# The small addition of 1e-9 to the softmax sums: on GpSimd instead of VectorE

## The chip, the core and the metric

The kernel runs on one core of a Trainium2 chip. The core has five engines with instruction queues of their own: TensorE (PE in the profile, its weight loads PEld), VectorE (DVE), ScalarE (ACT), GpSimd (POOL) and SyncE (SP, which here issues the DMAs). Each engine works through its queue in order, and engines wait for each other by semaphores. The metric is the device time of one execution in microseconds, lower is better.

## The reference

Sink attention with a sliding window feeds a layer of experts. The first part, with 4 batches, 8 heads, 768 positions and head size 64:

```python
scores = scale * np.matmul(q, k.transpose(0, 1, 3, 2))
keep = is_sink | in_window            # 4 sinks, window of 128
scores = np.where(keep, scores, -1e9)
scores = scores - np.max(scores, axis=-1, keepdims=True)
a = np.exp(scores)
a = a / (np.sum(a, axis=-1, keepdims=True) + 1e-09)
attn = np.matmul(a, v)
```

The second part takes the 3072 x 512 result `x`, forms gates `P` from `x @ w_gate` by eight rounds of row and column normalisation, and adds up eight experts: `out += P[:, e:e+1] * (relu(x @ w1[e]) @ w2[e])`.

## The kernel before

**Attention.** The work is cut into 48 units: 4 batches x 6 blocks of 128 positions x 2 halves of the heads, so a unit has 4 heads. A unit's scores are 128 queries by 260 columns a head: 4 sinks, the block before and the block itself. Values are split into a rounded part and a rest, so most products are three matmuls. The loop over `n` (lines 712 to 756) interleaves units: in round `n`, PE makes the scores of unit `n + 1`, transposes the queries and keys of unit `n + 2`, transposes the probabilities of unit `n`, and multiplies those of `n - 1` with the values. Between them it does pieces of the first expert (`run_fill`, `gate_step`).

**The work around the change** is in `scores(n, pr)`, called twice a unit, for heads 0 and 1 and for heads 2 and 3:

- L461, PE: six matmuls into two PSUM tiles of the pool `ps_st`, which has four;
- L464, DVE: scale, mask and row minimum of the negated scores, once a head;
- L467, ACT: the exponential, once a head; its row sums go to `sm`;
- L468: add 1e-9 to the two columns of sums, giving `rs` (128 partitions x 2);
- L469, DVE: the reciprocal of `rs`, in place;
- L471, GpSimd: multiply the 128x260 probabilities of each head by its column of `rs`.

Other lines that the prediction names: L430 and L431 split the transposed queries and keys (ACT rounds, DVE takes the rest); L350 is the same split for several things, among them the transposed probabilities `PT` and pieces of weights (`W`, `W2f`); L482 is PE's transpose of the probabilities; L604 and L605 are the activation of the first expert's hidden layer; L440 and L441 split `v` on GpSimd; L496 and L497 split the sinks' probabilities there; L403, L406 and L407 prepare the sinks' values once a batch; L532 copies the finished output, L540 and L541 split it.

The four tiles of `ps_st` are used eight times a round: four for scores, one for the transposed queries and keys, two for the transposed probabilities, one for the sinks. So a round's scores can be written only when L431, L350 and L501 of the round before have read their tiles.

**What sets the order.** In this stage only PE's order is the order of the code (`tc.manual_schedule(engines={PE})`, line 711). On DVE, ACT and GpSimd the framework's planner orders the instructions, by their place in the program and by its own estimate of when each can start. From line 1140 on all engines follow the code's order, and L468 does not occur any more.

**Afterwards** come the gates' normalisation, interleaved with the first expert, and then the experts' products for the rest of the span, in a form that needs seven block products where the plain one has eight.

Of the kernel before, what the change touches and what calls it, by code (L numbers as in the profile page):

```python
# [12 lines left out]
ALU = mybir.AluOpType  # L13
# [216 lines left out]
def tile_sink_attention_moe(ctx: ExitStack, tc: tile.TileContext, q, k, v, wg, w1, w2, out):  # L230

    nc = tc.nc
# [211 lines left out]
    def scores(n, pr):  # L444

        b, i, hh = units[n]
        u = us[n]
        K, Q = KQ[hh][:, :, :, 0:CW], KQ[hh][:, :, :, CW:][:, :, :, turn_of(b, i)]
        if pr == 0:
            u["sc"] = att.tile([P, HH, CW], F32, name="sc", bufs=3)  # L450
            u["st"] = att.tile([P, 3, HH], F32, name="st", bufs=3)
        sc = u["sc"]
        nmx, sm, rs = (u["st"][:, j, :] for j in range(3))
        hs = range(2 * pr, 2 * pr + 2)
        p2 = slice(2 * pr, 2 * pr + 2)
        ps = {h: ps_st.tile([P, CW], F32, name="st") for h in hs}

        for j, (a, c) in enumerate(((0, 0), (0, 1), (1, 0))):
            for h in hs:
                r0 = (h % 2) * D  # L460
                nc.tensor.matmul(ps[h], lhsT=Q[r0:r0 + D, a, pr, :], rhs=K[r0:r0 + D, c, pr, :],  # L461
                                 start=(j == 0), stop=(j == 2))
        for h in hs:
            nc.vector.tensor_tensor_reduce(out=sc[:, h, :], in0=ps[h], in1=masks[place(b, i).start, min(i, 2)], op0=ALU.add, op1=ALU.min,  # L464
                                           scale=-scale, scalar=3.0e38, accum_out=nmx[:, h:h + 1])
        for h in hs:
            nc.scalar.activation(sc[:, h, :], sc[:, h, :], AF.Exp, bias=nmx[:, h:h + 1], scale=-1.0, accum_out=sm[:, h:h + 1])  # L467
        nc.vector.tensor_scalar(rs[:, p2], sm[:, p2], 1e-9, None, op0=ALU.add)  # L468
        nc.vector.reciprocal(rs[:, p2], rs[:, p2])  # L469
        for h in hs:  # L470
            u["scaled"] = nc.gpsimd.tensor_scalar(sc[:, h, :], sc[:, h, :], rs[:, h:h + 1], 1.0, op0=ALU.mult, op1=ALU.mult).ins  # L471
# [239 lines left out]
    with tc.manual_schedule(engines={PE}):  # L711
        for n in range(-2, L + 3):
# [15 lines left out]
            if on(n + 1):  # L728
                scores(n + 1, 0)
                scores(n + 1, 1)  # L730
# [788 lines left out]
```

## Time and profile before

| | |
|---|---|
| time, median of 3 runs | 2141.11 us (2140.84 to 2141.45) |
| the profiled execution's own time | 2141.32 us |
| its span (first to last instruction) | 2139.5 us |
| busy in the span: PE, DVE, ACT, POOL | 2120.6, 1538.2, 883.0, 752.4 us |
| mean granted TensorE clock | 0.998 |

The times in the profile are those of one execution, in microseconds from the start of the span unless marked ns. A timeline row has the start, the duration, the engine, the line of the code, the operation, the tiles (written <- read) and a count; in brackets stands how long the engine was idle before it and who ended that. Consecutive instructions on one engine overlap a little, as the next starts before the one in front has written its last result. A row by line has a count and the smallest, median and largest duration in ns. A row of windows gives the stretch, its length, then busy time and count of PE, PEld, DVE, ACT and POOL, the granted clock, the share of DMA and GB/s. A row of the chain has the start, the time on the chain, the engine, tile and line.

### The profile page before, as it was taken

To read this page: it belongs to the slowest core of one execution; us is meant where nothing else is said; L and a number is where in the kernel's file an instruction comes from. 1 tells how busy PE (TensorE), PEld (TensorE's weight loads), DVE (VectorE), ACT (ScalarE), POOL (GpSimd) and SP (SyncE) were. 2 spreads that over 40 slices of the span, in tenths; PEclk is the share of its full clock that TensorE was granted. 3 is DMA by queue.
4 is the path that set the end of the run, shared out by engine and by line. 5 is a ranking of instruction groups with operands and counts; after the bars stand their busy time and mean duration, and the time that the engine had idled before them with its cause. 6 is when DMAs were issued, how large, how long until landed. Compare 5 with 4: busy or idle time off the path is not lost.

```text
span 2139.5 us, 31828 instructions
## 1 busy us (share of the span) xinstructions
PE 2120.6 (99%) x10501; PEld 1770.4 (83%) x10501; DVE 1538.2 (72%) x2821; ACT 883.0 (41%) x1867; POOL 752.4 (35%) x950
## 2 busy tenths in 40 slices
PE   8999999999999999999999999999999999999998
PEld 7898897888888888888888888888888888888887
DVE  9878878877777776766666666666656666676666
ACT  7777744444444444442333223332333223332222
POOL 7766643233232331232223222232423232233223
PEclk9999999999999999999999999999999999999999
DMA  7434326999998987686666666667866666666662
GB/s 184 96 81 103 85 80 223 320 300 315 295 315 286 313 287 251 219 278 209 201 191 204 206 193 205 202 200 260 300 205 194 200 206 193 201 207 189 205 197 85
DMA packets 397643, 453.83 MB, mean 212 GB/s; under 512 B 99680, under 2 KB 265760, under 8 KB 396576
## 3 DMA queue, kind: packets, MB, share of 16 engines
q1 hardware_dynamic: 397080, 451.57, 67.8%
q8 instruction: 86, 1.41, 0.3%
q14 instruction: 85, 0.70, 0.1%
q10 hardware_dynamic: 392, 0.16, 0.0%
HBM read 314.17 MB, written 137.46 MB: 211 GB/s over the span
## 4 chain that ended last, share of the span: by engine, by line
PE 93%; DVE 3%; ACT 2%; POOL 1%; issue 0%; DMA 0%; SPq 0%; DVEq 0%; ACTq 0%; POOLq 0%
PE c L784 41%; PE o L1343 20%; PE held L1343 8%; PE o L1028 7%; PE held L1028 7%; PE O L520 3%; PE st L461 2%; ACT sc L467 1%; PE o L615 1%; PE st L482 1%; PE g L599 1%; PE st L426 1%; DVE sc L464 0%; POOL sc L471 0%; DVE PT L350 0%
## 5 line engine op out<-in xcount | busy, mean ns | idle before, releaser
L810 ACT CAST hf<-w 128x512 fp32r<-128x512 f32 x448 | 265.5, 622 | 561.8 <-POOL w L1310 298.9
L1343 PE MATMUL o<-hf,W2q 128*128 128x512 f32 x1920 | 472.0, 389 | 0.0
L1343 PEld LDWEIGHTS o<-hf,W2q 128*128 128x128 f32 x1920 | 360.0, 188 | 75.5 <-DVE acc L1357 0.9
L784 PE MATMUL c<-T,W1q 128*128 128x512 f32 x1530 | 388.9, 389 | 0.2 <-DVE w L1291 0.2
L811 DVE TENSOR_TENSOR hf<-w,hf 128x512 fp32r<-128x512 f32 x448 | 329.3, 763 | 76.2 <-ACT hf L810 68.5
L784 PEld LDWEIGHTS c<-T,W1q 128*128 128x128 f32 x1530 | 286.8, 188 | 60.7 <-DVE w L1291 0.9
L1357 DVE TENSOR_TENSOR acc<-o,acc 128x512 f32<-128x512 f32 x298 | 204.7, 688 | 171.1 <-PE o L1343 171.1
L784 PE MATMUL c<-B,W1q 128*128 128x512 f32 x1134 | 278.3, 389 | 0.0
L1310 POOL TENSOR_TENSOR w<-w 128x512 f32<-128x512 f32 x64 | 82.7, 1293 | 491.6 <-DVE w L1292 491.6
L784 PEld LDWEIGHTS c<-B,W1q 128*128 128x128 f32 x1134 | 212.5, 188 | 44.0
L1291 DVE TENSOR_TENSOR w<-c,M 128x512 f32<-128x512 f32 x192 | 132.3, 689 | 138.0 <-PE c L784 132.6
L1287 ACT COPY M<-c 128x512 f32<-128x512 f32 x192 | 112.7, 587 | 249.4 <-PE c L784 249.3
L1343 PE MATMUL held<-hf,W2q 128*128 128x512 f32 x768 | 194.8, 389 | 0.0
L784 PE MATMUL c<-T,W1f 128*128 128x512 f32 x672 | 171.2, 390 | 0.1
L1028 PE MATMUL held<-W2f,h 128*128 128x512 f32 x672 | 171.1, 390 | 0.0
L1028 PE MATMUL o<-W2f,h 128*128 128x512 f32 x672 | 170.6, 389 | 0.1
L1343 PEld LDWEIGHTS held<-hf,W2q 128*128 128x128 f32 x768 | 144.0, 188 | 29.8
L1325 POOL TENSOR_TENSOR w<-w 128x512 f32<-128x512 f32 x64 | 106.3, 1661 | 176.0 <-DVE hf L811 176.0
L1028 PEld LDWEIGHTS o<-W2f,h 128*128 128x128 f32 x672 | 126.0, 188 | 27.0 <-DVE acc L1035 0.9
L784 PEld LDWEIGHTS c<-T,W1f 128*128 128x128 f32 x672 | 125.7, 188 | 27.0 <-issue 0.5
L1028 PEld LDWEIGHTS held<-W2f,h 128*128 128x128 f32 x672 | 125.8, 188 | 26.4 <-DVE W2f L811 0.5
L837 POOL TENSOR_TENSOR r<-r 128x256 f32<-128x256 f32 x27 | 20.1, 746 | 359.2 <-ACT M L991 223.1
(216 smaller groups left out, 3104.5 us busy)
## 6 DMA issues: line engine op xcount, KB each, us to landing
W2q<-w2s SPq DMA_DIRECT2D x448, 256.0 KB, 3.2
W1q<-w1s SPq DMA_DIRECT2D x444, 256.0 KB, 2.9
w1s<-W1f SPq DMA_DIRECT2D x56, 896.0 KB, 7.8
w2s<-WT SPq DMA_DIRECT2D x136, 256.0 KB, 3.5
r<-in_moe_w_dram SPq DMA_DIRECT2D x64, 512.0 KB, 3.9
w2s<-W2f SPq DMA_DIRECT2D x56, 256.0 KB, 4.8
PB<-psd SPq DMA_DIRECT2D x16, 512.0 KB, 4.1
w2s<-W2f SPq DMA_DIRECT2D x56, 128.0 KB, 6.5
```

The source lines that it names most:

```text
L461: nc.tensor.matmul(ps[h], lhsT=Q[r0:r0 + D, a, pr, :], rhs=K[r0:r0 + D, c, pr, :], start=(j == 0), stop=(j == 2))
L520: nc.tensor.matmul(u["O"][:, pr], lhsT=x_, rhs=y_, start=(j == 0), stop=(j == len(ops) - 1))
L784: nc.tensor.matmul(ps, lhsT=w1(a, k), rhs=x[:, b, k, :], start=(start and j == 0), stop=(stop and j == len(TERMS) - 1), skip_group_check=n ...
L810: nc.scalar.copy(dst[:, 0], src)
L811: at(1, lambda: nc.vector.tensor_sub(dst[:, 1], src, f32(dst[:, 0])))
L1028: nc.tensor.matmul(o, lhsT=h[c, th][:, a, off:off + P], rhs=W2F[n][:, w, c, :], start=(begin and c == 0 and j == 0), stop=(end and c == 1 ...
L1287: nc.scalar.copy(t, T["c2"])
L1291: nc.vector.tensor_add(w, T["c1"], T[m])
L1310: nc.gpsimd.tensor_sub(S3, T["A11"], T["A21"])
L1325: at(k, lambda: nc.gpsimd.tensor_sub(T["A11"], w, T["A11"]))
L1343: nc.tensor.matmul(o, lhsT=W2Q[part, n, m][:, a, k * P:(k + 1) * P], rhs=F[part, n, H_OF[m]][:, w, :], start=(j == 0 and (begin or not hol ...
L1357: nc.vector.tensor_add(sums[m, k], o, sums[m, k])
```

## The change

The addition at L468 goes from VectorE to GpSimd. There it is written with a second operation, a multiplication by 1.0, which leaves the value as it is. The reciprocal after it stays on VectorE and the scaling on GpSimd. Nothing else is edited.

```diff
         for h in hs:
             nc.scalar.activation(sc[:, h, :], sc[:, h, :], AF.Exp, bias=nmx[:, h:h + 1], scale=-1.0, accum_out=sm[:, h:h + 1])
-        nc.vector.tensor_scalar(rs[:, p2], sm[:, p2], 1e-9, None, op0=ALU.add)
+        nc.gpsimd.tensor_scalar(rs[:, p2], sm[:, p2], 1e-9, 1.0, op0=ALU.add, op1=ALU.mult)
         nc.vector.reciprocal(rs[:, p2], rs[:, p2])
         for h in hs:
             u["scaled"] = nc.gpsimd.tensor_scalar(sc[:, h, :], sc[:, h, :], rs[:, h:h + 1], 1.0, op0=ALU.mult, op1=ALU.mult).ins
```

## The prediction

> **What bounds the kernel now.** I read the page's chain of work that ended last first; then the windows that cut the span into stages; then inside the attention stage the views of single lines and the list of waits from 60 us on, the timeline of one steady round, and the chain of the first 44 us.
>
> ```profile
> PE 93%; DVE 3%; ACT 2%; POOL 1%; issue 0%; DMA 0%; SPq 0%; DVEq 0%; ACTq 0%; POOLq 0%
> ...
> 8.00:30.00 22.00, 19.39 (x107) 15.71 (x107) 20.85 (x80) 17.09 (x55) 18.48 (x40) 0.92 0.80 203
> 30.00:60.00 30.00, 28.70 (x247) 26.21 (x245) 27.83 (x100) 26.30 (x83) 21.85 (x53) 1.00 0.64 168
> ...
> 110.00:160.00 50.00, 50.00 (x431) 45.47 (x432) 38.51 (x142) 35.58 (x111) 29.01 (x69) 1.00 0.36 85
> ...
> L468 DVE TENSOR_SCALAR st<-st x96: 140/170/1282, 10.1 to 288.5; 128x2 f32<-128x2 f32 x96
> DVE KQ L431 <- ACT KQ L430: 3.8, 11, 1.0
> L431 DVE TENSOR_TENSOR KQ<-st,KQ x38: 670/692/694, 60.4 to 283.4; 128x512 fp32r<-128x512 f32 x38
> ```
>
> TensorE (PE) carries 93% of the chain, so time is lost or won only where PE waits. The window rows list busy time of PE, PEld, DVE, ACT and POOL. L468, the changed addition, runs 96 times, all before 289 us: the other 1850 us of the span have none of it and can only shift as a block. Within the first 289 us there are two stages. From 8 to 60 us VectorE (DVE) is busy 20.85 of 22 and 27.83 of 30 us: there it is as much the limit as PE. From 110 to 160 us PE is busy for all 50 us while DVE has 11 us free and GpSimd (POOL) 21 us: there PE is the limit. The last two rows, from 60 us on, are the waits of L431 and its count: 38 rounds, in 11 of which it waits for L430 on ScalarE (ACT); they come up below.
>
> One steady round, DVE first, then GpSimd, ACT and PE's weight loads:
>
> ```profile
> 120.03 0.17 DVE L468 TENSOR_SCALAR st<-st 128x2 f32<-128x2 f32 x1
> 120.24 0.17 DVE L469 RECIPROCAL st<-st 128x2 f32<-128x2 f32 x1
> 121.02 0.17 DVE L468 TENSOR_SCALAR st<-st 128x2 f32<-128x2 f32 x1 [0.62 <-ACT sc L467]
> 121.23 0.17 DVE L469 RECIPROCAL st<-st 128x2 f32<-128x2 f32 x1
> 121.31 0.41 DVE L605 SCALAR_TENSOR_TENSOR h<-g,h 128x256 fp32r<-128x256 f32 x1
> 121.76 0.69 DVE L431 TENSOR_TENSOR KQ<-st,KQ 128x512 fp32r<-128x512 f32 x1
> 122.37 1.28 DVE L350 TENSOR_TENSOR PT<-st,PT 128x512 fp32r<-128x512 f32 x2
> 120.58 1.93 POOL L471 TENSOR_SCALAR sc<-sc,st 128x260 f32<-128x260 f32 x4 [3.96 <-ACT sc L467]
> 119.81 0.19 ACT L467 ACTIVATION_READ_ACCUMULATOR sc<-sc,st 128x1 f32 x1
> 121.16 0.57 ACT L430 CAST KQ<-st 128x512 fp32r<-128x512 f32 x1
> 123.25 0.87 PEld L461 LDWEIGHTS st<-KQ 64*128 64x128 f32 x12 [0.37 <-DVE PT L350]
> 127.00 0.51 PEld L482 LDWEIGHTS st<-ident,sc 128*128 128x128 f32 x4
> ```
>
> A round does a pair of heads twice. The first pair's sums are ready at 119.81 + 0.19 = 120.00, which I call e. DVE adds, divides and ends at 120.41, and GpSimd scales from 120.58, e + 0.58. The second pair's sums come at e + 0.99; DVE had stood 0.62 us waiting for them. What follows on DVE is what PE needs: L431 and L350, whose results free the PSUM tiles that PE's next scores (L461) write. L431 starts at 121.76, e + 1.76, just after ACT's cast L430 ends at 121.16 + 0.57 = 121.73. In 11 rounds of 38 it even stands waiting for that cast. So in the steady stage the addition is not what L431 waits for.
>
> **The change, part by part.** Removed: 96 DVE instructions of 0.17 us median. Added: 96 GpSimd instructions of the same shape. Moved: the wait for ACT goes from DVE's queue to GpSimd's, and DVE's reciprocal L469 now waits for GpSimd, with L605, L431 and L350 queued behind it. On GpSimd the scalings L471 and then the splits of v (L440, L441) and of the sinks (L496, L497) are queued behind the addition; PE uses these a round or more later. No DMA is issued or moved.
>
> *The price of the addition on GpSimd.* The trace has no 128x2 addition there. The nearest rows are L496, 128x16, at 0.205 us, and on the far side a GpSimd fill of 128x4 at 0.10 us.
>
> ```profile
> L496 POOL TENSOR_SCALAR SS<-sc x80: 201/205/216, 21.6 to 290.3; 128x16 fp32r<-128x16 f32 x80
> L287 POOL MEMSET mask<- 128x4 f32 x1 | 0.1, 100 | 0.0
> 77.03 0.41 ACT L540 CAST B<-xr 128x256 fp32r<-128x256 f32 x1 [1.02 <-DVE xr L532]
> 77.52 0.74 POOL L541 TENSOR_TENSOR B<-xr,B 128x256 fp32r<-128x256 f32 x1 [0.28 <-ACT B L540]
> 81.81 0.74 POOL L441 TENSOR_TENSOR V<-vr,V 128x256 fp32r<-128x256 f32 x1
> 82.60 0.43 DVE L464 CUSTOM_DVE_ANT_0 sc<-st,mask 128x260 f32<-128x260 f32 x1 [0.16 <-POOL V L441]
> ```
>
> I take 0.20 us, the same kind of instruction; the ends are 0.10 and 0.22. The handovers are in the last four rows: ACT to GpSimd 77.52 − 77.44 = 0.08 us, GpSimd to DVE 82.60 − 82.55 = 0.05 us. DVE to GpSimd is 120.58 − 120.41 = 0.17 us already. The first pair then goes: e + 0.08, addition to e + 0.28, reciprocal e + 0.33 to e + 0.50, scaling from e + 0.67. That is 0.09 us later than e + 0.58: nothing, as GpSimd had been idle 3.96 us before.
>
> *The second pair* decides. Its sums come at e + 0.99, but GpSimd is then in the first pair's two scalings (4 take 1.93, so 0.48 each) until e + 0.67 + 0.97 = e + 1.64. The addition ends at e + 1.84, the reciprocal can start at e + 1.89, while L431 has its cast at e + 1.76. Which of the two comes first in DVE's order is not written in the kernel: only PE's order is. The trace shows how the framework's planner places things:
>
> ```profile
> 31.39 0.14 DVE L468 TENSOR_SCALAR st<-st 128x2 f32<-128x2 f32 x1
> 31.52 0.69 DVE L431 TENSOR_TENSOR KQ<-st,KQ 128x512 fp32r<-128x512 f32 x1
> 32.12 0.15 DVE L469 RECIPROCAL st<-st 128x2 f32<-128x2 f32 x1
> ```
>
> It already puts L431, where that is ready, between the addition and its reciprocal. With the addition an engine away, I expect the second reciprocal behind L431 in most rounds. Then it costs DVE its step, 121.31 − 121.23 = 0.08 us, ahead of L350. Of the 38 steady rounds, 27 show no wait ahead of L431 and so have no room: 27 x 0.08 = **+2.2 us**; the ends are 0 and 38 x 0.08 = 3.0. The scaling of the second pair ends some 0.7 us later than before; before, it ended at 120.58 + 1.93 = 122.51, and PE's transposes of it (L482, the last row) start at 127.00, so 4.5 us of room cover it. Without that room the 0.7 would be paid in each of the 38 rounds, 27 us.
>
> *The first 44 us.* Here the addition does stand on the chain:
>
> ```profile
> 16.65 1.28 DVE L468 TENSOR_SCALAR st<-st 128x2 f32<-128x2 f32 x1
> 17.18 0.73 POOL L441 TENSOR_TENSOR V<-vr,V 128x256 fp32r<-128x256 f32 x1
> 17.99 1.27 POOL L407 TENSOR_TENSOR VS<-vm,VS 32x512 fp32r<-32x512 f32 x1
> 18.05 1.23 DVE L468 TENSOR_SCALAR st<-st 128x2 f32<-128x2 f32 x1
> 19.41 0.67 DVE L431 TENSOR_TENSOR KQ<-st,KQ 128x512 fp32r<-128x512 f32 x1
> 17.70 0.59 ACT L430 CAST KQ<-st 128x512 fp32r<-128x512 f32 x1
> by line: DVE sc L464 15.3%; DVE st L468 10.2%; ACT sc L467 9.1%; POOL sc L471 8.4%; PE st L461 6.7%; DVE KQ L431 5.2%; PE O L520 5.2%; DVE PT L350 5.2%; PE st L482 5.0%; DVE W2f L350 4.3%; issue 3.9%; DVE W L350 3.9%; DVE wgr L310 3.2%; PE
> ```
>
> L468 is 10.2% of 36 us of chain, 3.7 us. Two of them last 1.28 and 1.23 us instead of 0.17, and end (17.93, 19.28) within 0.02 us of the GpSimd instructions beside them (17.91, 19.26): the small addition is held until GpSimd's instruction is done. The Trainium skill, "SBUF — State Buffer", section "Who interferes with whom", says that a VectorE tensor_scalar can take a port pair that GpSimd also uses, and that the one that comes second is blocked for the whole of the other. The rows agree. Without them L431 could start when its cast ends, 18.29, instead of 19.41: −1.1 us. Of the other 3.7 − 2.5 = 1.2 us I take −0.9. If instead the addition is queued behind L407 and the reciprocals stay ahead of L431, it ends 19.46 for the first pair, two scalings and a second addition follow, and L431 starts at about 20.7: +1.3. I take **−2.0 us**, ends −3.7 and +1.3.
>
> Sum: 2141.32 (the profiled run: span 2139.5 and 1.8 around it) + 2.2 − 2.0 = 2141.5. That run lies 0.2 above the median of 2141.11, so I say **2141.3**.
>
> **The rivals.** A measurement of this kernel can tell about 0.2%, 4.3 us, from no change.
>
> *DVE stands behind GpSimd* (slower). The second reciprocal stays ahead of L431, and DVE, whose queue is in order, waits for it: L431 at e + 1.89 + 0.08 = e + 1.97 instead of e + 1.76: +0.21. For it speaks that the planner already lets DVE stand 0.62 us at L468 for ACT, so its timing is not the chip's. That is 38 x 0.21 = 8.0 if PE feels it in every round, 27 x 0.21 = 5.7 in those without room: about +7, 2148. It decides from the point at which the reciprocal, ready at e + 1.89, is placed ahead of L431.
>
> *A packed GpSimd* (slower). Once per batch GpSimd runs L403, L406 and L407, and an addition behind L407 waits up to 1.27 us with the reciprocal and all of DVE behind it: 4 x 1.3 = +5.2, 2146.5. Against it: such work is later in the program than the scores' own.
>
> *VectorE is freed* (faster).
>
> ```profile
> 90.38 0.41 DVE st L468
> 233.22 0.35 DVE st L468
> ```
>
> All of the 3.7 us come off, and the later places where the chain, read to its end, runs through the addition: three, the first and the last of which are shown, about 1.1 us. That makes −4.8, 2136.5. Against it: from 110 us on L431 waits for ACT, not for DVE. The Trainium skill, "Perfetto Trace Analysis", section "Optimizing Scalar/DVE Operations", warns that moving work between VectorE and GpSimd may not help, as they share a port; by that this rival would give nothing.
>
> **How the numbers follow.** Forecast 0.54, within 0.2%. DVE behind GpSimd 0.25, of which 0.04 stay within 0.2%. Packed GpSimd 0.06, slower. VectorE freed 0.15, of which 0.02 within. So faster 0.13, same 0.60, slower 0.27. The range goes from the faster rival, 2136, to just above the slower one, 2149.
>
> **What would show it.** Right: GpSimd additions near 0.2 us; on DVE, L431 ahead of the second L469; L468's long stalls gone; the end of attention near 290 us as before. Wrong: DVE idle ahead of L469 with GpSimd as releaser in most rounds, PE waiting longer for L350 or L431, and the last scaling later than 289.5 us by several us.

## The result and the profile after

The changed kernel takes 2167.94 us (median; 2167.03 to 2170.15) against 2141.2 us (2140.84 to 2141.45): a ratio of 1.0127, 95% interval 1.0109 to 1.0144. It is 27 us slower; the forecast was 2141.3, with 2149 as the upper end.

The chain that ended last, by engine, and the three windows of before, now of the changed kernel (length, busy time of PE, PEld, DVE, ACT, POOL, granted clock, DMA share, GB/s):

```profile
PE 91%; DVE 3%; POOL 2%; ACT 1%; issue 1%; DMA 0%; ACTq 0%; POOLq 0%; DVEq 0%
```

```profile
8.00:30.00 22.00, 16.93 (x82) 13.69 (x82) 13.42 (x57) 13.65 (x45) 16.96 (x38) 0.86 0.79 189
30.00:60.00 30.00, 24.96 (x198) 21.03 (x197) 24.21 (x78) 22.48 (x68) 23.20 (x58) 0.99 0.52 141
110.00:160.00 50.00, 50.00 (x414) 44.50 (x414) 34.01 (x118) 35.18 (x112) 32.35 (x89) 1.00 0.36 85
```

PE's share of the chain went from 93 to 91%. In the first two windows PE is busy 16.93 and 24.96 us, where it had been 19.39 and 28.70; DVE fell from 20.85 and 27.83 to 13.42 and 24.21. So DVE is not relieved there, it stands. In the third window PE is still "busy" for all 50 us, but with 414 matmuls instead of 431: the window covers less of the program.

Where DVE stands is in the list of waits (waiting instruction, releaser, us in total, times, longest). First the row of the changed kernel over the whole span and its addition, then PE's wait for L431 up to 330 us, and the same row of the kernel before:

```profile
DVE st L469 <- POOL st L468: 84.6, 87, 2.6
```

```profile
L468 POOL TENSOR_SCALAR st<-st x96: 191/192/476, 10.6 to 315.7; 128x2 f32<-128x2 f32 x96
```

```profile
PEld st L461 <- DVE KQ L431: 22.3, 23, 2.9
```

```profile
PEld st L461 <- DVE KQ L431: 6.9, 13, 0.9
```

The addition itself takes 0.192 us on GpSimd, close to the 0.20 of the prediction. But in 87 of 96 cases DVE stands at the reciprocal until it is done, 84.6 us in all, and PE's wait for the split behind it grew from 6.9 to 22.3 us.

By how much each round is late can be read at L431, which runs once a round. Its rows by line, before and after, show the last of the 48:

```profile
L431 DVE TENSOR_TENSOR KQ<-st,KQ x48: 668/692/694, 5.8 to 283.4; 128x512 fp32r<-128x512 f32 x48
```

```profile
L431 DVE TENSOR_TENSOR KQ<-st,KQ x48: 668/672/692, 5.9 to 310.1; 128x512 fp32r<-128x512 f32 x48
```

From 5.9 to 310.1 instead of 5.8 to 283.4: the 48 rounds hold the whole loss of 26.7 us, and from there on the program is only shifted. The difference of the starts, round by round, is the measure of every experiment below. I cut it in three: the **start** (rounds 1 to 10), the **packed rounds** (16, 17, 28, 29, 40 and 41, in which GpSimd has the sinks' values, L403, L406 and L407, and what follows on them) and the **other 32 rounds**. In the changed kernel these lost 8.7, 8.8 and 9.2 us.

One steady round of the changed kernel, a timeline of DVE, then of GpSimd and of ACT:

```profile
134.63 0.17 DVE L469 RECIPROCAL st<-st 128x2 f32<-128x2 f32 x1 [0.46 <-POOL st L468]
136.15 0.17 DVE L469 RECIPROCAL st<-st 128x2 f32<-128x2 f32 x1 [1.35 <-POOL st L468]
136.23 0.40 DVE L605 SCALAR_TENSOR_TENSOR h<-g,h 128x256 fp32r<-128x256 f32 x1
136.55 0.68 DVE L431 TENSOR_TENSOR KQ<-st,KQ 128x512 fp32r<-128x512 f32 x1
```

```profile
134.40 0.19 POOL L468 TENSOR_SCALAR st<-st 128x2 f32<-128x2 f32 x1 [3.41 <-ACT sc L467]
134.89 0.94 POOL L471 TENSOR_SCALAR sc<-sc,st 128x260 f32<-128x260 f32 x2 [0.30 <-DVE st L469]
135.92 0.19 POOL L468 TENSOR_SCALAR st<-st 128x2 f32<-128x2 f32 x1
```

```profile
134.13 0.19 ACT L467 ACTIVATION_READ_ACCUMULATOR sc<-sc,st 128x1 f32 x1
...
135.12 0.19 ACT L467 ACTIVATION_READ_ACCUMULATOR sc<-sc,st 128x1 f32 x1
135.21 0.36 ACT L604 ACTIVATE h<-g 128x256 fp32r<-128x256 f32 x1
135.48 0.57 ACT L430 CAST KQ<-st 128x512 fp32r<-128x512 f32 x1
```

With e = 134.13 + 0.19 = 134.32 as before: the second pair's sums are there at 135.12 + 0.19 = 135.31, but its addition starts at 135.92, right behind the first pair's two scalings. The second reciprocal starts at 136.15, e + 1.83. L605 and L431 stand behind it, and L431 starts at e + 2.23, where it had been e + 1.76; its cast had been done at 136.05.

From round 13 on, only every second round has L604 on ACT and L605 on DVE. In the others ACT comes to the cast sooner, as in this one (e = 140.83):

```profile
141.72 0.56 ACT L430 CAST KQ<-st 128x512 fp32r<-128x512 f32 x1
142.74 0.67 DVE L431 TENSOR_TENSOR KQ<-st,KQ 128x512 fp32r<-128x512 f32 x1
```

The cast is done at 142.28, e + 1.45, and L431 starts at e + 1.91, right behind the second reciprocal.

And the start of the program, same engines:

```profile
19.34 1.27 POOL L407 TENSOR_TENSOR VS<-vm,VS 32x512 fp32r<-32x512 f32 x1
20.70 0.19 POOL L468 TENSOR_SCALAR st<-st 128x2 f32<-128x2 f32 x1
20.92 0.17 DVE L469 RECIPROCAL st<-st 128x2 f32<-128x2 f32 x1 [2.39 <-POOL st L468]
22.44 0.17 DVE L469 RECIPROCAL st<-st 128x2 f32<-128x2 f32 x1 [1.35 <-POOL st L468]
22.52 0.67 DVE L431 TENSOR_TENSOR KQ<-st,KQ 128x512 fp32r<-128x512 f32 x1
```

Here the first pair's addition waits behind L407 and the second's behind the first pair's scalings. DVE stands 2.39 and 1.35 us, and L431 starts at 22.52 instead of 19.41.

### The profile page after: what moved, and what is told of

Read it like the earlier page. It is cut to its first block, busy times and chain, and to the rows that moved or that the text cites. A ratio compares the mean times of both kernels' runs of the same rounds, so it can differ in the third digit from the quotient of the medians.

```text
span 2166.4 us, 31805 instructions
## 1 busy us (share of the span) xinstructions
PE 2134.7 (99%) x10501; PEld 1779.1 (82%) x10501; DVE 1517.0 (70%) x2725; ACT 882.5 (41%) x1867; POOL 773.3 (36%) x1046
## 4 chain that ended last, share of the span: by engine, by line
PE 91%; DVE 3%; POOL 2%; ACT 1%; issue 1%; DMA 0%; ACTq 0%; POOLq 0%; DVEq 0%
PE c L784 40%; PE o L1343 20%; PE held L1343 8%; PE held L1028 7%; PE o L1028 7%; PE O L520 2%; PE st L461 2%; PE o L615 1%; PE g L599 1%; PE st L482 1%; ACT sc L467 1%; POOL sc L471 1%; DVE PT L350 1%; PE st L426 1%; DVE KQ L431 0%
```

## The experiments

**Theory.** What costs is the place in GpSimd's queue: the second pair's addition stands behind the first pair's two scalings, or any addition behind other GpSimd work, and the planner leaves the reciprocal ahead of L605 and L431 on DVE. **Rivals.** The hop between the engines costs by itself, whatever the order; the extra load on GpSimd costs, or the hold between small DVE instructions and the GpSimd instruction beside them that the prediction read at 16.65 and 18.05 us; the loss is one of the start and of a few packed rounds, and the rest only carries it on.

All runs, against the kernel before on the same chip (medians of 2140.6 to 2141.2). The three columns on the right are the lateness of L431 gained in the parts named above, in us; they add up to the lateness of the 48th round. They are those of one profiled execution: for load_only they add up to 2.6, while its median is 3.8 above (its ten executions took 2143.0 to 2146.2).

| kernel | median us | ratio, 95% interval | start | packed | other 32 |
|---|---|---|---|---|---|
| changed | 2167.94 | 1.0127 (1.0109 to 1.0144) | +8.7 | +8.8 | +9.2 |
| pair0 | 2144.41 | 1.0017 (1.0007 to 1.0027) | +1.6 | +2.3 | −0.6 |
| pair1 | 2158.23 | 1.0083 (1.0067 to 1.0100) | +2.7 | +6.1 | +8.4 |
| load_only | 2144.51 | 1.0019 (1.0009 to 1.0029) | +0.2 | 0.0 | +2.4 |
| no_add | 2139.03 | 0.9991 (0.9981 to 1.0000) | −1.4 | −0.2 | −0.1 |
| adds_first | 2147.67 | 1.0033 (1.0020 to 1.0045) | +1.9 | +4.3 | +0.4 |
| recip_late | 2157.63 | 1.0082 (1.0065 to 1.0099) | +6.2 | +7.8 | +2.5 |
| recip_mid | 2155.86 | 1.0071 (1.0054 to 1.0088) | +4.1 | +8.3 | +1.7 |
| sinks_later | 2152.37 | 1.0056 (1.0039 to 1.0073) | +1.9 | +6.9 | +2.4 |
| steady_after | 2150.34 | 1.0046 (1.0029 to 1.0062) | −0.1 | +0.1 | +10.1 |
| steady_first | 2141.87 | 1.0005 (0.9995 to 1.0014) | −0.3 | +2.0 | −0.7 |
| steady_mid | 2145.50 | 1.0021 (1.0012 to 1.0031) | +0.2 | +3.7 | +0.3 |

### One pair at a time: pair0 and pair1

Only the first pair's addition goes to GpSimd, or only the second's (`pr == 1`):

```diff
-        nc.vector.tensor_scalar(rs[:, p2], sm[:, p2], 1e-9, None, op0=ALU.add)
+        if pr == 0:
+            nc.gpsimd.tensor_scalar(rs[:, p2], sm[:, p2], 1e-9, 1.0, op0=ALU.add, op1=ALU.mult)
+        else:
+            nc.vector.tensor_scalar(rs[:, p2], sm[:, p2], 1e-9, None, op0=ALU.add)
```

> Only the first pair's addition of each unit on GpSimd, the second's on VectorE. Theory (queue): the loss is VectorE's wait at the second reciprocal, whose addition stands behind two scalings in GpSimd's queue; here that wait is gone, so 2141 to 2149 us, what is left over coming from the few rounds where an addition stands behind the sinks' work (L403 to L407). Rival (engine hop): each addition on GpSimd costs its longer way to the reciprocal and back, the first pair as much as the second: about half of the 27 us, 2152 to 2156. Rival (GpSimd load and port): half the added GpSimd work, again about half, 2152 to 2156.

> Only the second pair's addition on GpSimd, the first's on VectorE. Theory (queue): the second addition still stands behind the two scalings of the first pair, VectorE still waits about 1.3 us at the second reciprocal of a round: most of the 27 us stay, 2155 to 2168. Rivals (engine hop, or load and port): about half, 2152 to 2156, the same as the kernel with only the first pair moved.

Measured: 2144.41 and 2158.23. The first pair's hop costs nothing in the other 32 rounds (−0.6 us): DVE stands 0.46 us for it there, but in time that it had. The second pair's alone makes +8.4 there, nearly the changed kernel's +9.2. So an engine hop as such has no price in the steady rounds; the hop behind the scalings has. What pair0 does lose comes in single rounds, like this one, of which DVE and GpSimd are shown (its reciprocal is L472):

```profile
91.09 1.28 POOL L407 TENSOR_TENSOR VS<-vm,VS 32x512 fp32r<-32x512 f32 x1
92.44 0.73 POOL L544 TENSOR_TENSOR B<-xr,B 128x256 fp32r<-128x256 f32 x1
93.26 0.19 POOL L469 TENSOR_SCALAR st<-st 128x2 f32<-128x2 f32 x1
93.48 0.17 DVE L472 RECIPROCAL st<-st 128x2 f32<-128x2 f32 x1 [2.61 <-POOL st L469]
```

The addition stands behind L407 and another split, 1.28 + 0.73 us of work that has nothing to do with it, and DVE with all behind it stands 2.61 us. The two losses do not simply add: 3.7 + 17.5 = 21.2 us is less than the 27 of both together.

### The load without the wait: load_only

DVE keeps its addition; GpSimd does the same addition once more, into a column that nobody reads:

```diff
-            u["st"] = att.tile([P, 3, HH], F32, name="st", bufs=3)
+            u["st"] = att.tile([P, 4, HH], F32, name="st", bufs=3)
...
         nc.vector.reciprocal(rs[:, p2], rs[:, p2])
+        nc.gpsimd.tensor_scalar(u["st"][:, 3, p2], sm[:, p2], 1e-9, 1.0, op0=ALU.add, op1=ALU.mult)
```

> The kernel before, with VectorE's addition as it was, and beside it the same addition on GpSimd a second time, into a row that nobody reads. GpSimd has all the added work, and VectorE waits for none of it. Theory (queue): VectorE's wait is what costs, so 2140 to 2145 us. Rival (load and port): the work itself delays the scalings or blocks VectorE, 2155 to 2168.

Measured: 2144.51, +3.8 us. The whole load of 96 additions on GpSimd, with nobody waiting for them, costs a seventh of the loss, and by a path that the changed kernel doesn't have. In a steady round:

```profile
121.04 0.94 POOL L472 TENSOR_SCALAR sc<-sc,st 128x260 f32<-128x260 f32 x2 [0.23 <-DVE st L469]
121.56 0.45 DVE L468 TENSOR_SCALAR st<-st 128x2 f32<-128x2 f32 x1 [0.62 <-ACT sc L467]
```

DVE's second addition takes 0.45 us instead of 0.17 and ends at 122.01, just after GpSimd's two scalings (121.98): it is held by the GpSimd instruction beside it. In the changed kernel this addition is no longer on DVE.

### The addition left out: no_add

```diff
-        nc.vector.tensor_scalar(rs[:, p2], sm[:, p2], 1e-9, None, op0=ALU.add)
-        nc.vector.reciprocal(rs[:, p2], rs[:, p2])
+        nc.vector.reciprocal(rs[:, p2], sm[:, p2])
```

> Leaves out the addition of 1e-9 altogether; the reciprocal reads the sums. Shows what the addition on VectorE was worth, the most that moving it away could have won. Theory (queue): in the steady rounds L431 waits for ScalarE, so only the start can win: 2137 to 2141.5 us. Rival (VectorE is the limit, as in the third rival of the prediction): 2134 to 2137.

Measured: 2139.03, −1.7 us, and the interval reaches to no change. From round 11 on nothing is won. In the start the long stalls go, and L431 of round 4 waits for its cast again, as the prediction had read it:

```profile
17.59 0.69 DVE L431 TENSOR_TENSOR KQ<-st,KQ 128x512 fp32r<-128x512 f32 x1 [0.41 <-ACT KQ L430]
```

That is 1.8 us earlier than 19.41, but rounds later only 1.4 of it is left. This is the most that any move of the addition off DVE can bring. "VectorE is freed", with its −4.8 us, was not there to be had.

### Both additions ahead of the scalings: adds_first

The two additions stay on GpSimd; the four scalings of a unit are placed behind the second addition:

```diff
+        added = nc.gpsimd.tensor_scalar(rs[:, p2], sm[:, p2], 1e-9, 1.0, op0=ALU.add, op1=ALU.mult).ins
         nc.vector.reciprocal(rs[:, p2], rs[:, p2])
-        for h in hs:
+        if pr:
+            with tc.issue_after(added):
+                for h in range(HH):
...
```

> Both additions on GpSimd as in the changed kernel, but a unit's four scalings are put behind its second addition in GpSimd's queue. All the moved work and all the handovers stay; only the order on one engine differs, and the first pair is scaled about 0.7 us later. Theory (queue): the second reciprocal is ready before L431 has its cast from ScalarE, so the loss of the steady rounds (0.4 to 0.6 us in most rounds with L605 or a cast early enough) and most of the start go; what stays are the four rounds in which the additions stand behind the sinks' work: 2142 to 2149 us. Rival (engine hop): every handover is still there, so at least 2155. Rival (load): the same work, so about 2162 to 2168.

Measured: 2147.67. Only the order on GpSimd was edited against the changed kernel, and 20 of the 27 us are gone. (On DVE the planner moved a reciprocal past other work in three rounds, in none of them past L431.) A steady round (L607 is L605 of before):

```profile
124.39 0.19 POOL L468 TENSOR_SCALAR st<-st 128x2 f32<-128x2 f32 x1 [3.41 <-ACT sc L467]
125.37 0.19 POOL L468 TENSOR_SCALAR st<-st 128x2 f32<-128x2 f32 x1 [0.79 <-ACT sc L467]
```

```profile
124.61 0.17 DVE L469 RECIPROCAL st<-st 128x2 f32<-128x2 f32 x1 [0.46 <-POOL st L468]
125.59 0.17 DVE L469 RECIPROCAL st<-st 128x2 f32<-128x2 f32 x1 [0.82 <-POOL st L468]
125.68 0.40 DVE L607 SCALAR_TENSOR_TENSOR h<-g,h 128x256 fp32r<-128x256 f32 x1
126.06 0.69 DVE L431 TENSOR_TENSOR KQ<-st,KQ 128x512 fp32r<-128x512 f32 x1
```

With ACT's handover of 0.08 us, e is 124.39 − 0.08 = 124.31. The second reciprocal starts at e + 1.28 and L431 at e + 1.75, as early as before the change. DVE still stands 0.46 + 0.82 us a round for GpSimd, and that costs nothing: the same kind of wait is free at e + 1.28 and costs L431 0.47 us at e + 1.83. What remains is +1.9 in the start and +4.3 in the packed rounds; the next experiment but one asks whether that is L407.

### The reciprocal behind L431: recip_late and recip_mid

GpSimd's order stays that of the changed kernel, but the second reciprocal is placed on DVE behind L431: in recip_late behind L350 too, in recip_mid between the two, which is exactly the order that the prediction expected of the planner. The lines of recip_mid (`lo` is the instruction of L431):

```diff
+    def scale_late(n, after):
+        u = us[n]
+        sc, rs = u["sc"], u["st"][:, 2, :]
+        with (tc.issue_after(after) if after is not None else nullcontext()):
+            u["recip"] = nc.vector.reciprocal(rs[:, 2:4], rs[:, 2:4]).ins
...
                 if on(j):
                     transpose_qk(j)
+            if on(n + 1):
+                scale_late(n + 1, us[n + 2]["lo"] if on(n + 2) and n >= 0 else None)
             if on(n):
```

> Both additions on GpSimd in the changed kernel's order there, with the second addition behind the first pair's scalings; on VectorE the second reciprocal is put behind L431 and L350, as the prediction had assumed it would be. Theory (queue): what hurts is that L431 and L350 stand behind the waiting reciprocal; behind them it costs only its own step, so 2141 to 2149 us, with the rounds behind the sinks' work left over. Rival (the scaling comes too late for the transposes): the second pair is then scaled some 1.5 us later than in the changed kernel, and PE waits at L482: no better than 2160.

> The order that the prediction expected, exactly: all additions on GpSimd as in the changed kernel, the second reciprocal on DVE right behind L431 and ahead of L350 (in the run named recip_late it stood behind L350 too). Theory (a late reciprocal pushes GpSimd's scalings and splits, and with them the next round's additions, into DVE's way; at 0.6 us a piece less late than there, GpSimd stands less): better than the 2157.6 of recip_late, but the start and the packed rounds still lose 6.7 or more together as in adds_first, so 2148 to 2155, with the other 32 rounds within 2.5 us. Rival (the prediction's reading: this order costs 0.08 us in 27 rounds and relieves the start): 2139 to 2144.

Measured: 2157.63 and 2155.86, the first a miss, the second 0.9 us above its range. The other 32 rounds get most of their loss back (+2.5 and +1.7 against +9.2), and in recip_mid a steady round looks as predicted, L431 at its cast and L350 a step of 0.07 us behind the reciprocal (L478; DVE's timeline):

```profile
147.25 0.69 DVE L431 TENSOR_TENSOR KQ<-st,KQ 128x512 fp32r<-128x512 f32 x1 [1.17 <-ACT KQ L430]
147.86 0.15 DVE L478 RECIPROCAL st<-st 128x2 f32<-128x2 f32 x1
147.93 1.27 DVE L350 TENSOR_TENSOR PT<-st,PT 128x512 fp32r<-128x512 f32 x2
```

But the start and the packed rounds still lose 14.0 and 12.4 us together, where the changed kernel had 17.5. There the wait has changed sides. In recip_late, where it is plainest, GpSimd's list of waits (L480 are the second pair's scalings) and a stretch of its and DVE's timeline (L470 is the first reciprocal, L550 the split L541 of before):

```profile
POOL sc L480 <- DVE st L478: 59.2, 47, 2.5
```

```profile
121.44 0.75 POOL L550 TENSOR_TENSOR B<-xr,B 128x256 fp32r<-128x256 f32 x1
122.46 0.19 POOL L468 TENSOR_SCALAR st<-st 128x2 f32<-128x2 f32 x1
122.68 0.17 DVE L470 RECIPROCAL st<-st 128x2 f32<-128x2 f32 x1 [1.67 <-POOL st L468]
```

GpSimd stands 59.2 us for the late reciprocal (30.4 in recip_mid), its splits slide into the next round, and there the *first* pair's addition comes behind them: DVE stands 1.67 us at a reciprocal that used to wait 0.46. So with the order of the prediction, forced in this way, the change still costs 15 us.

### The sinks' work a round later: sinks_later

As adds_first, with the sinks' values prepared behind the scalings of the next unit:

```diff
-                with tc.issue_after(us[n]["scaled"]):
+                with tc.issue_after(us[n + 1]["scaled"]):
                     split_sinks
```

> As the kernel with the additions first, and besides the sinks' work of a batch (L403, L406, L407) stands behind the scalings of the next unit, a round later, so that no addition waits behind it in the first round of a batch. Theory (queue): the steps of 1.3, 0.5 and 0.5 us that the kernel with only the first pair moved shows in the first rounds of the batches (rounds 16, 28, 40) go, and 2139.5 to 2144 us are left, within 0.2% of the kernel before. Rival: those steps come from something else in these rounds (their shorter PE work leaves less room), and the time stays that of the kernel with the additions first.

Measured: 2152.37, a miss too. Rounds 16, 28 and 40 lose nothing any more (0.0 us each), but 17, 18, 29 and 41 lose 2.8, 2.1, 2.1 and 2.1. GpSimd and DVE in round 17:

```profile
97.83 1.27 POOL L407 TENSOR_TENSOR VS<-vm,VS 32x512 fp32r<-32x512 f32 x1
99.17 0.72 POOL L543 TENSOR_TENSOR B<-xr,B 128x256 fp32r<-128x256 f32 x1
99.98 0.46 POOL L468 TENSOR_SCALAR st<-st 128x2 f32<-128x2 f32 x2
100.20 0.44 DVE L469 RECIPROCAL st<-st 128x2 f32<-128x2 f32 x2 [4.04 <-POOL st L468]
```

In the packed rounds the loss goes where the sinks' work goes. That settles what it is made of there, though not how to avoid it; the 1.9 us of the start stay and are not tested.

### The steady rounds alone: steady_after, steady_first, steady_mid

The addition goes to GpSimd only in the 33 units outside the start and the packed rounds, once as in the changed kernel, once with the order of adds_first, once with that of recip_mid:

```diff
-        nc.vector.tensor_scalar(rs[:, p2], sm[:, p2], 1e-9, None, op0=ALU.add)
+        if n >= 9 and n % 12 not in (2, 3):
+            nc.gpsimd.tensor_scalar(rs[:, p2], sm[:, p2], 1e-9, 1.0, op0=ALU.add, op1=ALU.mult)
+        else:
+            nc.vector.tensor_scalar(rs[:, p2], sm[:, p2], 1e-9, None, op0=ALU.add)
```

> The addition goes to GpSimd in the changed kernel's form, but only in 33 of 48 units: not in the first nine, and not in the two of each batch whose rounds carry the sinks' values; there it stays on VectorE. Theory (in the steady rounds the second pair's addition stands behind the first pair's two scalings in GpSimd's queue, and DVE stands at the reciprocal with L605 and L431 behind it): the losses of after in just these rounds add up to about 9.3 us, so 2150, with 0.4 to 0.6 us in rounds that have L605 and little in the others. Rival (the loss of after is one of the start and of the packed rounds, and the later rounds only carry it on): 2141 to 2143.

> The same 33 units, with both additions of a unit on GpSimd ahead of its four scalings. Theory (queue position alone): no loss in the steady rounds, none in the start and the packed rounds as these are as before: 2140.5 to 2142.5, no worse than before. Rival (each wait of DVE for GpSimd costs by itself, by the handover or the port): at least half of the other form's loss stays, 2145 or more.

> The same order in the 33 units outside the start and the packed rounds alone, the other units as before the change. Prediction's step: a step of 0.08 us ahead of L350 in each round, at most +3 us, 2141 to 2144. Theory: DVE no longer stands ahead of L431, so no more than that, 2141 to 2144, as GpSimd has room in these rounds to be 0.7 us later. Rival (the delay of GpSimd comes back as a wait of DVE at the next round's first reciprocal): 2145 or more.

Measured: 2150.34, 2141.87 and 2145.50. The first gives back the start and the packed rounds in full (−0.1 and +0.1) and keeps +10.1 in the others, where the changed kernel had +9.2: so these are losses of their own and not carried on. Where they lie was expected wrongly: 6.0 of the 10.1 are gained in the 17 rounds without L605, 4.1 in the 15 with it. In the second, the time as a whole can't be told from no change, though the packed rounds, in which nothing was moved, still show +2.0.

The third splits the prediction's order in two. In the 32 other rounds it costs +0.3 us, as the theory and the prediction's step have it. Its +4.9 in all is the rival's number, though: +3.7 come from the packed rounds, in which nothing was moved. So the delay of GpSimd does come back, but not as a wait for a reciprocal. Round 16, DVE and then GpSimd (L472 is DVE's addition there, L554 the split L541 of before):

```profile
89.93 1.61 DVE L472 TENSOR_SCALAR st<-st 128x2 f32<-128x2 f32 x1 [0.18 <-ACT sc L467]
91.66 1.22 DVE L472 TENSOR_SCALAR st<-st 128x2 f32<-128x2 f32 x1
```

```profile
89.52 0.62 POOL L406 TENSOR_SCALAR VS<-vm 96x512 fp32r<-96x512 f32 x1
90.10 0.73 POOL L441 TENSOR_TENSOR V<-vr,V 128x256 fp32r<-128x256 f32 x1
90.80 0.72 POOL L554 TENSOR_TENSOR B<-xr,B 128x256 fp32r<-128x256 f32 x1
91.60 1.25 POOL L407 TENSOR_TENSOR VS<-vm,VS 32x512 fp32r<-32x512 f32 x1
```

The round before has left GpSimd late, so its splits now lie beside DVE's two additions, and hold them to 91.54 and 92.88, the ends of L554 (91.52) and of L407 (92.85). A delay on GpSimd thus reaches DVE even where no semaphore joins the two. In steady_first the second addition of this round is held in the same way, 1.03 us beside L407, where it took 0.40 before the change.

No version with the addition on GpSimd came out faster than the kernel before.

## Why the prediction was wrong

**The durations and the timing held.** The addition was put at 0.20 us and takes 0.192; the second reciprocal was to be ready at e + 1.89 and starts at e + 1.83. The first pair's addition was put at nothing in the steady rounds; pair0 shows −0.6 us in the other 32. That the addition isn't what L431 waits for in the steady stage holds as well: without it, no_add wins 0.1 us there. And the price of the expected order in the steady rounds, +2.2, was if anything too high: steady_mid has +0.3 in them.

**The step that failed** is "I expect the second reciprocal behind L431 in most rounds". In the changed kernel the planner left both reciprocals ahead of L431 in all 46 rounds that have them (3 to 48), and, but for one, ahead of L605; so DVE stood at the second reciprocal for its addition, 84.6 us in 87 waits for both pairs. The evidence was the place at 31.39 us where L431 had slipped between an addition and its reciprocal. The trace of before has four such rounds in a row (L431 at 26.00, 31.52, 37.12 and 42.83), all in the start, and none in the 40 rounds behind them, of which the forecast used it for 38. They show that the planner can do it, not that it will. The rival "DVE stands behind GpSimd" had named the mechanism and its deciding point, but got 0.25. Its price was too small as well: +0.21 a round for L431, where the round above shows e + 2.23 against e + 1.76, +0.47: it had left out that L605, 0.40 us on DVE, stands in the same queue and is no longer done during the wait. And it took this kind of round for all. In the rounds without L605 the cast is done sooner, before the change mostly at e + 1.46 to e + 1.62, so the same late reciprocal costs more than 0.21 there too: in 15 of these 17 rounds L431 goes from e + 1.49 to 1.65 to e + 1.91 or later, and the 17 hold 6.4 of the 9.2 us. So "about +7" came out as +9.2 in the other 32 rounds.

**The order that the prediction counted on was no cover either.** The whole forecast rested on it, at +2.2 − 2.0; recip_mid, which forces it, costs 15.2, of which 12.4 lie in the start and the packed rounds. The prediction had followed DVE's queue, and of GpSimd's only that PE uses its results late. It had not asked what a delay of GpSimd does to the next round's addition once that is in GpSimd's queue.

**The first 44 us** were put at −2.0, ends −3.7 and +1.3. They came out at +7.4 by round 8, where they end, and +8.7 by round 10. The case of +1.3 was read correctly, L407 ahead of the addition and two scalings ahead of the next one, but for one round alone. In this stage DVE was busy 27.83 of 30 us, so the waits are paid for: L431 falls behind by 0.5 to 2.4 us in each of the rounds 3 to 10. With the order of adds_first 1.9 of it remain, so 6.8 came from the second addition's place behind the scalings.

**The packed GpSimd** was a rival of 4 x 1.3 = +5.2 with a chance of 0.06. It was real, and of about that size: of the +8.8 in the six packed rounds, adds_first leaves +4.3, in three batches. The rest is the second addition behind the scalings, there as elsewhere. The argument against it, that such work is later in the program than the scores' own, said nothing about where it stands when a sum becomes ready.

**The rivals were treated as alternatives; all three slow cases happened together**: 7 + 5.2 + 1.3 = 13.5 by their own prices, and twice that in fact. By the runs, 20 of 27 us are the second addition behind the first scalings (adds_first). Of the other 7, the 4.3 of the packed rounds are additions behind L407 and the splits around it (sinks_later); for the 1.9 of the start that is argued from the rows, not tested.

On the pages: the Trainium skill, "Perfetto Trace Analysis", section "Optimizing Scalar/DVE Operations", says that offloading between VectorE and GpSimd might not help because of the port. The outcome is worse than that, and the port can't be much of it: load_only, with that load and no wait, costs 3.8 us, and adds_first, with the load and the handovers, 6.8 of 27. The Trainium skill, "PSUM — Partial Sum Buffer", section "Engine vs sequencer instructions", calls the queues of these engines strictly first in, first out; this rule decided here, and the rows of the steady round agree (ready at 135.31, started at 135.92 behind the scalings).

## What to carry to other kernels

Before moving a link of a chain to another engine, don't ask how long it takes there but what stands ahead of it in that engine's queue at the moment when it is ready, and what then stands behind its successor on the engine that it left. A producer that is followed by a consumer on the same GpSimd queue delays the next producer by that consumer: do the small links of all groups first, the large ones after. And when a planner sets the order, several orders are possible in each round: work out the bad one for every round and add its costs up, for they are not exclusive.

## What was not expected of the hardware

DVE's small addition is at the mercy of GpSimd's phase. In the steady round of before, it starts at 121.02, as GpSimd's first scaling runs out (121.06) and 0.02 us ahead of the second (121.04), and takes 0.17 us. In load_only, where this round is 0.54 us later as a whole, GpSimd's scalings start at e + 0.50 instead of e + 0.58, 0.08 us earlier against the rest. The second scaling is this one:

```profile
121.50 0.48 POOL L472 TENSOR_SCALAR sc<-sc,st 128x260 f32<-128x260 f32 x1
```

It is 0.06 us ahead of the addition at 121.56, which takes 0.45 us, to just past the scaling's end. Additions of over 0.22 us go from 13 of 96 to 46 of 96, and the 32 other rounds lose 2.4 us: a shift of less than a tenth of a microsecond on one engine lengthens an instruction on another that waits for nothing that the program states. The rule of the Trainium skill, "SBUF — State Buffer", section "Who interferes with whom", which the prediction cites, fits these rows; which port the addition took is not shown by them. In steady_mid's round 16 the hold outlasts one instruction: the addition at 89.93 came while L406 ran, and was kept waiting through L441 and L554, which followed without a gap, 1.61 us for a 128x2 operation. The turn did not come to DVE between them. The prediction's row of 1.28 us at 16.65 was such a case already: it starts 0.53 us ahead of the L441 beside it, and is held through the L406 that ran before that one as well (16.60 to 17.21). This is no general rule: over all runs seven holds of the addition on DVE outlast the first GpSimd instruction by 0.7 us or more, and each of them runs past the end of L406; in 30 others the next GpSimd instruction follows as closely, and the addition ends with the first. Why L406 differs is not shown.
